# Attention and two MLPs on one Trainium2 core: weight parts of the second block pair kept in DRAM, a later touch ahead of three loads, and Silu in place of tanh for part of the first MLP

## The chip, the cores and the metric

The kernel runs on one core of a Trainium2 chip. The metric is the device time of one execution, in microseconds (us). The engines are named as the profile names them: PE is TensorE's matmul, PEld its weight load, DVE is VectorE, ACT is ScalarE, POOL is GpSimd, and SP is SyncE, which here only issues transfers (DMAs).

## What is computed

A landmark (Nystrom) attention for 4 batches, 8 heads, 576 tokens and head size 64; then a gated MLP with an RMS norm (512 to 1536 and back) and an MLP with squared ReLU (512 to 2048 and back) on all 2304 rows, in fp32.

```python
def _attn_ref(q, k, v):          # B, H, S, D = 4, 8, 576, 64; m = 32 landmarks
    q_lm = q.reshape(B, H, m, S // m, D).mean(axis=3)
    k_lm = k.reshape(B, H, m, S // m, D).mean(axis=3)
    A, Bm, C = sm(q, k_lm), sm(q_lm, k_lm), sm(q_lm, k)   # softmax of scaled products
    Z = Bm.transpose(0, 1, 3, 2) / (norm1(Bm) * norminf(Bm) + 1e-06)
    for _ in range(6):
        Z = 2 * Z - Z @ Bm @ Z
    return A @ Z @ C @ v

def _moe_ref(x, w_gate, w_val, w_out, rms_g):
    xn = x / np.sqrt(np.mean(x * x, axis=-1, keepdims=True) + 1e-06) * rms_g
    g = xn @ w_gate
    return (g * (1.0 / (1.0 + np.exp(-g)))) * (xn @ w_val) @ w_out

def _moe2_ref(x, w_in, w_out, s, b):
    r = np.maximum(x @ w_in, 0.0)
    return (s * (r * r) + b) @ w_out
```

## The kernel before, in words

**Order.** The code does not issue instructions as it is written. Each step is given to a `Scheduler` (`op`, L128) with the engines that may do it, a duration by formula, a due time (`key`) and what it reads and writes. `Scheduler.run` (L185) plays this plan once, on the host, and issues the instructions of each engine in the order that comes out; on the chip an engine then works strictly in that order and waits by semaphore. So a change of a duration, a due time or a buffer can move instructions on every engine.

**Stages.** Attention of batch 0 runs alone (to about 43 us); PE has little real work there, and plain matmuls on ones fill its gaps. From 43 to 406 us the first MLP of batch 0, 1, 2, 3 runs, and the attention of the next batch is woven into it. The first MLP's output product runs on to about 447 us. From about 416 us the second MLP begins: its 2304 rows are four blocks of 512 and one of 256, and the blocks are taken as two pairs (`pairs`, L459). From about 781 us the last block's output product ends the program.

**fp32 as two halves.** Large products are done on a rounded high part and the remainder, three matmuls for each product (`PART3`). `split` (L1228) makes both: a copy to the high part (ACT or DVE, L1230/L1231) and a subtraction (DVE or POOL, L1232).

**First MLP.** `fused` (L1419) multiplies the attention's small factor into the weights and evicts the result from two PSUM banks (L1441 to L1444). `hidden` (L1467) does, for each of 96 pieces of 128x288: the gate product into bank `pg`, ACT's `Tanh` of half of it (L1473), DVE's (tanh + 1) * gate (L1475, which reads `pg` again), the value product into `pv`, and DVE's 0.5 * that * value (L1479). Tanh and Exp share one ACT table here; the plan knows two table names, "tanh" and "sqrt", and charges `TABLE` = 1.28 us on a change. `out_mm` (L1486) is the output product, with weights loaded from DRAM (`kepto`) into a ring of two `rawo` buffers by `out_weights` (L1307).

**Second MLP, first layer.** Each pair of blocks goes through seven half-size products instead of eight (`PRODUCTS`, L1731), for 8 groups `g` of output columns (`group_of`, L1769). For this each group needs the weights' parts: three raw quarters and four sums and differences, each split in two halves. `sums` (L1382) makes them in both pairs alike: a load of 512 KB (`in_weights`, L1376), two splits into `raw` (128x1536), four differences of 128x256 (`difference`, L1327), two splits into `tot` (128x2048). `raw` and `tot` have two slots each.

**Second MLP, second layer.** `output` does the first pair and the last block; `output7` (L1875) does the second pair in seven products, with loads of stored weights: `kept5` goes straight into the weight tile `w_all`, `region` or `u_all` by a DMA on POOL's queue (L1880), `kept4` by SP.

**Start.** SP issues q, k, v of batch 0 and then the first weights. `load_gains` (L531) loads the RMS gains; on SP's queue the next loads stand behind it, a `w_val` and a `w_gate` piece first. It waits for `touch` (L535), a dummy matmul on PE that reads `gT`, and that one for the product `pY` (L766).

Of the kernel before, what the change touches and what calls it, by code (L numbers as in the profile page):

```python
# [59 lines left out]
DWELL, DWELL_FROM = 2.5, 145  # L60
ROW2, N_OUT, N_ONLY, OUT_ONLY, N_LAST = 4.0, 4.0, 4.0, 3, 1.6
# [55 lines left out]
class Scheduler:  # L117
# [67 lines left out]
    def run(self, warm):  # L185
# [10 lines left out]
        table = "tanh"  # L196
        while left:
# [61 lines left out]
            if e == "act" and o.table and o.table != table:  # L259
                table = o.table  # L260
                end += TABLE
            for b, s in self.slots_for(o).items():
                b.slot = s
                s.held = True
                if b.ring.queue:
                    b.ring.queue.remove(b)
# [36 lines left out]
def t_act(n):  # L303
    return 0.055 + 0.00085 * n
# [19 lines left out]
def tile_nystrom_attention_two_mlps(  # L324
# [131 lines left out]
    def flat(x):  # L456
        return x.rearrange("p k n -> p (k n)")
# [98 lines left out]
    def attention(b, t0, t1):  # L556
# [209 lines left out]
        if first:  # L766
            at(("pe", 0.1), pos, lambda e: touch(gT), r=[pY, "const", "top"], w=["paced"])
            load_gains(["paced"])
# [168 lines left out]
        def weighted(g, eC, rec, rc, p0):  # L937
# [14 lines left out]
            at(("pe", 0.13), p0 + 0.04, lambda e: tr(e, [4]), r=[(eC, 1), "ident", (pE[1], "taken")], w=[pE[1]])  # L952

# [428 lines left out]
    def sums(key, p, g):  # L1382
        raw, tot = Buf(raw_r), Buf(sum_r)

        def get(x, c, d, i):
# [3 lines left out]
                 "S2": get(tot, 0, 1024, 0), "S4": get(tot, 256, 1024, 0), "S1": get(tot, 512, 1024, 1), "S3": get(tot, 768, 1024, 1)}  # L1389
        r = in_weights(key, g)  # L1390
# [9 lines left out]
        for i in (1, 0):  # L1400
            c = 512 * i
            split(key + 1, lambda c=c: tot.t[:, c:c + 512], lambda c=c: tot.t[:, 1024 + c:1536 + c],
                  lambda c=c: flat(r.t)[:, c:c + 512], [(r, 2 * i), (r, 2 * i + 1)], (tot, "h", i), (tot, "l", i), 512)
        return parts
# [62 lines left out]
    def hidden(tg, tv, b, f, hf, u):  # L1467
# [5 lines left out]
        op(("act", t_act(HC)), tg, lambda e: e.activation(  # L1473
            out=th.t[:, 0:HC], in_=pg.t[:, 0:HC], func=ACTF.Tanh, scale=0.5), r=[pg], w=[th]).table = "tanh"
        op(("dve", t_dve(HC)), tg, lambda e: e.scalar_tensor_tensor(  # L1475
            out=th.t[:, 0:HC], in0=th.t[:, 0:HC], scalar=1.0, in1=pg.t[:, 0:HC], op0=ALU.add, op1=ALU.mult),
            r=[pg, th], w=[th])
        first_mm(tv, b, 1, hf, u, pv)
        op(("dve", t_dve(HC)), tv, lambda e: e.scalar_tensor_tensor(  # L1479
            out=h.t, in0=th.t[:, 0:HC], scalar=0.5, in1=pv.t[:, 0:HC], op0=ALU.mult, op1=ALU.mult),  # L1480
# [387 lines left out]
    def output7(key, m, g):  # L1868
        nm, parts, (kd, d, c), ps = OUTS7[m]
        h, j = tiles[g], pairs[1]  # L1870
        if g % 2 == 0:
# [4 lines left out]
            def load(e):  # L1876
                for i, x in enumerate(src):
                    i = slice(256 * i, 256 * i + 256)
                    if kd == 5:
                        nc.gpsimd.dma_start(out=w.t.rearrange("p (y n) -> p y n", y=2)[:, :, i], in_=x[:, :, c].bitcast(F32R))  # L1880
# [198 lines left out]
```

## Time and profile before

| | us |
|---|---|
| median of 3 runs (lowest to highest) | 807.77 (804.77 to 807.83) |
| the profiled execution, its own time | 809.28 |
| span of its instructions | 807.3 |
| PE busy | 793.0 (98%) |
| DVE busy | 673.0 (83%) |
| ACT busy | 471.7 (58%) |
| POOL busy | 159.1 (20%) |
| moved by DMA | 151 MB, mean 187 GB/s |

The clock that PE was granted is full (2.4 GHz) in all slices but the last. The span is from the first to the last instruction; what lies around it in the profiled execution's own time is 2.0 us. A sum of differences is made against this span and carried over to the median.

### The profile page before, as it was taken

Reading aid. Unit: us, or ns where it says so; the run is one execution under the profiler, and the core shown is the slowest. Engines: PE = TensorE matmul, PEld = TensorE weight load, DVE = VectorE, ACT = ScalarE, POOL = GpSimd, SP = SyncE. Lnnn points to the kernel's source line nnn. Section 1 sums busy time; section 2 is a strip of 40 time slices with the busy share of each in tenths; the row PEclk is TensorE's granted clock in tenths of the full one; section 3 lists DMA queues with packets and bytes.
Section 4 is the critical chain, followed back from the end, with each engine's and each line's share of the span. In section 5 each row is a group of like instructions: output and inputs, shape, how many; then the busy total and the mean of one; then the engine's idle time right before and its main releaser. Section 6 shows DMA issues by size and latency. Waiting matters only on the chain.

```text
span 807.3 us, 17419 instructions
## 1 busy us (share of the span) xinstructions
PE 793.0 (98%) x6475; PEld 663.6 (82%) x6475; DVE 673.0 (83%) x1489; ACT 471.7 (58%) x1000; POOL 159.1 (20%) x224
## 2 busy tenths in 40 slices
PE   8899999999999999999999999999999999999997
PEld 6587777887788878888889888877788888999996
DVE  6889997888778877898998988889798789995674
ACT  5765744453334443565557856567665577857753
POOL 1263157127311143021000000012010120022000
PEclk9999999999999999999999999999999999999999
DMA  9899998653442332499888872121866851376352
GB/s 300 291 320 357 306 290 229 220 151 99 132 132 93 108 104 92 134 288 263 279 269 270 269 233 99 40 79 39 287 221 203 286 137 66 105 175 179 92 169 80
DMA packets 101413, 151.09 MB, mean 187 GB/s; under 512 B 29264, under 2 KB 66384, under 8 KB 101328
## 3 DMA queue, kind: packets, MB, share of 16 engines
q1 hardware_dynamic: 94656, 143.55, 56.0%
q0 software_dynamic: 6528, 6.29, 3.3%
q8 instruction: 51, 0.84, 0.4%
q14 instruction: 34, 0.28, 0.1%
q10 hardware_dynamic: 144, 0.13, 0.0%
HBM read 116.91 MB, written 33.03 MB: 186 GB/s over the span
## 4 chain that ended last, share of the span: by engine, by line
PE 78%; DVE 12%; DMA 5%; ACT 2%; issue 2%; SPq 0%; POOL 0%; DVEq 0%; ACTq 0%
PE bank L1456 16%; PE bank L1412 14%; PE bank L1520 14%; PE bank L1566 11%; PE bank L1907 10%; PE bank L1816 3%; PE bank L1429 3%; DMA rawo<-kepto 2%; DMA stage<-in_moe_w_in_dram 2%; DVE w_all L1232 1%; PE bank L830 1%; PE bank L746 1%; DVE hl L1232 1%; DVE region L1232 1%; PE bank L968 1%
## 5 line engine op out<-in xcount | busy, mean ns | idle before, releaser
L1520 PE MATMUL bank<-hh,w_all 128*128 128x512 f32 (+1 forms) x472 | 155.4, 381 | 0.0
L1520 PEld LDWEIGHTS bank<-hh,w_all 128*128 128x128 f32 x472 | 86.2, 188 | 27.2 <-issue 13.1
L1520 PE MATMUL bank<-hl,w_all 128*128 128x512 f32 (+1 forms) x236 | 87.5, 371 | 1.0 <-DVE hl L1232 1.0
L1456 PE MATMUL bank<-xh,u_all 128*128 128x288 f32 x400 | 86.9, 298 | 1.1 <-DVE hbuf L1475 0.7
L1566 PE MATMUL bank<-w_all,hh 128*128 128x512 f32 x272 | 83.9, 390 | 0.0
L1473 ACT ACTIVATE hbuf<-bank 128x288 f32<-128x288 f32 x96 | 39.2, 408 | 56.9 <-PE bank L1456 56.0
L1232 DVE TENSOR_TENSOR w_all<-rawo,w_all 128x512 fp32r<-128x512 f32 x83 | 60.2, 725 | 12.5 <-ACT w_all L1230 10.0
L1456 PEld LDWEIGHTS bank<-xh,u_all 128*128 128x128 f32 x400 | 66.1, 188 | 4.7 <-DVE hbuf L1475 1.1
L1566 PEld LDWEIGHTS bank<-w_all,hh 128*128 128x128 f32 x272 | 51.0, 188 | 10.9 <-ACT hh L1230 0.4
L1456 PE MATMUL bank<-xl,u_all 128*128 128x288 f32 x200 | 58.8, 294 | 0.0
L1456 PE MATMUL bank<-xh,xl 128*128 128x288 f32 x184 | 54.2, 294 | 0.0
L1456 PE MATMUL bank<-xl,xh 128*128 128x288 f32 x184 | 54.1, 294 | 0.0
L1566 PE MATMUL bank<-w_all,hl 128*128 128x512 f32 x136 | 53.0, 390 | 0.7 <-DVE hl L1232 0.7
L1475 DVE SCALAR_TENSOR_TENSOR hbuf<-hbuf,bank 128x288 f32<-128x288 f32 x96 | 42.6, 444 | 10.8 <-ACT hbuf L1473 10.8
L1520 PEld LDWEIGHTS bank<-hl,w_all 128*128 128x128 f32 x236 | 44.5, 189 | 6.6 <-POOL region L640 1.2
L1735 ACT ACTIVATE xbuf<-xbuf,b_sb,s_sb 128x512 f32<-128x512 f32 (+1 forms) x38 | 28.8, 758 | 20.9 <-DVE xbuf L1746 20.2
L1232 POOL TENSOR_TENSOR hl<-hbuf,hh 128x288 fp32r<-128x288 f32 (+7 forms) x32 | 23.3, 732 | 87.0 <-ACT hh L1230 64.6
L1230 ACT ACTIVATE hh<-hbuf 128x288 fp32r<-128x288 f32 (+8 forms) x74 | 27.4, 395 | 21.0 <-PE bank L1520 13.8
L1456 PEld LDWEIGHTS bank<-xl,u_all 128*128 128x128 f32 x200 | 37.6, 188 | 0.8
L1230 ACT ACTIVATE w_all<-rawo 128x512 fp32r<-128x512 f32 x45 | 28.2, 626 | 17.0 <-PE bank L1520 11.2
L1412 PE MATMUL bank<-region,xh 128*128 128x512 f32 x144 | 35.9, 394 | 0.6 <-ACT hbuf L1753 0.3
L1232 DVE TENSOR_TENSOR hl<-xbuf,hh 128x512 fp32r<-128x512 f32 (+5 forms) x45 | 27.9, 624 | 10.3 <-ACT hh L1230 9.5
(395 smaller groups left out, 2110.0 us busy)
## 6 DMA issues: line engine op xcount, KB each, us to landing
rawg<-keptg SPq DMA_DIRECT2D x36, 512.0 KB, 5.1
stage<-in_moe_w_out_dram SPq DMA_DIRECT2D x28, 511.8 KB, 5.5
rawo<-kepto SPq DMA_DIRECT2D x48, 256.0 KB, 3.4
rawg<-kept SPq DMA_DIRECT2D x24, 512.0 KB, 4.3
stage<-in_moe_w_in_dram SPq DMA_DIRECT2D x15, 512.0 KB, 5.0
rawo<-kept SPq DMA_DIRECT2D x27, 256.0 KB, 3.3
keptg<-rawg SPq DMA_DIRECT2D x12, 512.0 KB, 5.6
kept<-tail SPq DMA_DIRECT2D x24, 256.0 KB, 5.3
```

Of the source, the lines that this page charges most:

```text
L1230: e.activation(out=hi(), in_=src(), func=ACTF.Copy) if e is nc.scalar
L1232: b = op({"dve": t_dve(n), "pool": t_pool(n)}, key, lambda e: e.tensor_tensor(out=lo(), in0=src(), in1=hi().bitcast(F32), op=ALU.subtract) ...
L1412: nc.tensor.matmul(out=ps.t, lhsT=a[h][:, 128 * kd:128 * kd + 128], rhs=x[kd][y].t, start=(first and kd == 0 and i == 0), stop=(last and k ...
L1429: nc.tensor.matmul(out=pU[g].t[m, 256 * j:256 * j + 256], lhsT=gw[b].t[p, m], rhs=r.t[p, :, 128 * k:128 * k + 128], start=True, stop=True)
L1456: nc.tensor.matmul(out=ps.t[:, 0:HC], lhsT=u[a].t[:, 256 * g + 128 * part:256 * g + 128 * part + 128], rhs=x[y].t.rearrange("p k n -> p (k ...
L1473: op(("act", t_act(HC)), tg, lambda e: e.activation(out=th.t[:, 0:HC], in_=pg.t[:, 0:HC], func=ACTF.Tanh, scale=0.5), r=[pg], w=[th]).tabl ...
L1475: op(("dve", t_dve(HC)), tg, lambda e: e.scalar_tensor_tensor(out=th.t[:, 0:HC], in0=th.t[:, 0:HC], scalar=1.0, in1=pg.t[:, 0:HC], op0=ALU ...
L1520: nc.tensor.matmul(out=A[c].t[:, 0:n], lhsT=w[a].t[:, 128 * c:128 * c + 128], rhs=hs[y].t[:, 0:n], start=(f == 0 and i == 0), stop=(f == F ...
L1566: nc.tensor.matmul(out=A[c].t, lhsT=hs[a].t[:, s], rhs=w.t[:, 512 * y:512 * y + 512], start=(f == 0 and i == 0), stop=(f == F2 - 1 and i = ...
L1735: e.activation(out=h.t[:, c:c + n], in_=h.t[:, c:c + n], func=ACTF.Identity, scale=s_sb, bias=b_sb) if e is nc.scalar
L1816: nc.tensor.matmul(out=ps.t[:, 0:n], lhsT=tot.t[:, 1024 * a + c:1024 * a + c + 128], rhs=xs[3, kd // 2][y].t[:, n * (kd % 2):n * (kd % 2) ...
L1907: nc.tensor.matmul(out=A.t[:, 256 * k:256 * k + 256], lhsT=hs[x].t[:, t], rhs=w.t[:, 512 * y + w0:512 * y + w0 + 256], start=(fresh and k ...
```

## The change

Five edits:

1. `sums`: in the first pair every group's finished `raw` (768 KB) and `tot` (1 MB) are also stored to DRAM (`kept6`, `kept7`); in the second pair a group loads these two instead of the 512 KB of weights, and its splits and differences fall away.
2. `output7`: the `kept5` loads are issued by SP instead of POOL.
3. The touch ahead of the gains' load, and so the gains, a `w_val` and a `w_gate` piece behind it on SP's queue, waits for the transposes of the first attention half (`pE[1]`) instead of `pY`.
4. `hidden`: where the plan finds no exp near, ACT does `Silu` of the whole gate and DVE's (tanh + 1) * gate is not issued.
5. `Scheduler.run`: a third table name, "silu"; it changes to it when the sqrt table is in, when no exp is left, or when the next exps are not ready and not due soon. Each change is charged 1.28 us.

```diff
@@
+KEPT_LEAD = 4.0
+KEY0, EXP_AFTER = 39.0, 10.0
...
@@ Scheduler.run
+        self.exps = [o for o in self.ops if o.table == "tanh"]
...
-            if e == "act" and o.table and o.table != table:
+            if e == "act" and o.table == "silu":
+                if table != "silu" and (table == "sqrt" or not self.exps or (
+                        all(x.n_deps for x in self.exps) and min(x.key for x in self.exps) + KEY0 > at + EXP_AFTER)):
+                    table = "silu"
+                    end += TABLE
+                o.form(table == "silu")
+            elif e == "act" and o.table and o.table != table:
                 table = o.table
                 end += TABLE
+            if o in self.exps:
+                self.exps.remove(o)
...
@@ attention
         at(("pe", 0.26), pos, lambda e: diag(pY, 32, 32, block(BT), block(BT)), r=[BT], w=[pY])
-        if first:
-            at(("pe", 0.1), pos, lambda e: touch(gT), r=[pY, "const", "top"], w=["paced"])
-            load_gains(["paced"])
...
             at(("pe", 0.13), p0 + 0.04, lambda e: tr(e, [4]), r=[(eC, 1), "ident", (pE[1], "taken")], w=[pE[1]])
+            if first and g == 0:
+                at(("pe", 0.1), p0 + 0.04, lambda e: touch(gT), r=[pE[1], "const", "top"], w=["paced"])
+                load_gains(["paced"])
...
@@ sums
+        if p:
+            for i, x, n in ((6, raw, 1536), (7, tot, 2048)):
+                op(("sp", t_dma(n // 2)), key - KEPT_LEAD, lambda e, i=i, x=x: e.dma_start(out=x.t.bitcast(F32), in_=kept[i, g]),
+                   r=[("k%d" % i, g)], w=[(x, y, j) for y in "hl" for j in range(2)])
+            return parts
         r = in_weights(key, g)
...
+        for i, x, n in ((6, raw, 1536), (7, tot, 2048)):
+            kept[i, g] = dr.tile([128, n], F32, name=f"kept{i}_{g}")
+            op(("sp", t_dma(n // 2)), key + 8, lambda e, i=i, x=x: e.dma_start(out=kept[i, g], in_=x.t.bitcast(F32)),
+               r=[(x, y, j) for y in "hl" for j in range(2)], w=[("k%d" % i, g)])
         return parts
...
@@ hidden
-        op(("act", t_act(HC)), tg, lambda e: e.activation(
-            out=th.t[:, 0:HC], in_=pg.t[:, 0:HC], func=ACTF.Tanh, scale=0.5), r=[pg], w=[th]).table = "tanh"
-        op(("dve", t_dve(HC)), tg, lambda e: e.scalar_tensor_tensor(
+        o = op(("act", t_act(HC)), tg, lambda e: e.activation(
+            out=th.t[:, 0:HC], in_=pg.t[:, 0:HC], func=ACTF.Silu if silu else ACTF.Tanh, scale=1.0 if silu else 0.5),
+            r=[pg], w=[th])
+        o.table, silu = "silu", False
+        d = op(("dve", t_dve(HC)), tg, lambda e: None if silu else e.scalar_tensor_tensor(
             out=th.t[:, 0:HC], in0=th.t[:, 0:HC], scalar=1.0, in1=pg.t[:, 0:HC], op0=ALU.add, op1=ALU.mult),
             r=[pg, th], w=[th])
+
+        def form(x):
+            nonlocal silu
+            silu = x
+            if x:
+                d.alts = {"dve": 0.0}
+
+        o.form = form
...
-            out=h.t, in0=th.t[:, 0:HC], scalar=0.5, in1=pv.t[:, 0:HC], op0=ALU.mult, op1=ALU.mult),
+            out=h.t, in0=th.t[:, 0:HC], scalar=1.0 if silu else 0.5, in1=pv.t[:, 0:HC], op0=ALU.mult, op1=ALU.mult),
...
@@ output7
-                        nc.gpsimd.dma_start(out=w.t.rearrange("p (y n) -> p y n", y=2)[:, :, i], in_=x[:, :, c].bitcast(F32R))
+                        e.dma_start(out=w.t.bitcast(F32).rearrange("p (y n) -> p y n", y=2)[:, :, i], in_=x[:, :, c])
```

The built programs show what the plan makes of it. DVE: of 96 instructions of the kind (tanh + 1) * gate 34 stay; differences (L1328) fall from 131 to 104 on DVE and from 13 to 8 on POOL, subtractions of a split from 410 to 388 and from 63 to 53; DVE has 1376 instructions for 1491. ACT: seven `ACT_TABLE_LOAD` more (three for exp, four for Silu), 19 copies of a split fewer. SP: 16 stores and 24 + 16 loads more, 8 loads of 512 KB fewer. PE has the same products; one filling matmul falls away.

PE at the start, before: `tail` matmuls (L746) are `pY`, `ones` with `gT` is the touch, `ident` with `region` are the transposes.

```order
L746 MATMUL bank5_68<-tail_113 32x32 x8
L536 LDWEIGHTS ones_72
L536 MATMUL bank7_70<-gT_77,ones_72 128x128
L945 MATMUL bank4_67<-ident_71,region_109 128x128 x4
L945 MATMUL bank6_69<-ident_71,region_109 64x128
```

The same place now:

```order
L757 MATMUL bank5_68<-tail_113 32x32 x8
L953 MATMUL bank4_67<-ident_71,region_109 128x128 x4
L953 MATMUL bank6_69<-ident_71,region_109 64x128
L547 LDWEIGHTS ones_72
L547 MATMUL bank7_70<-gT_77,ones_72 128x128
```

The touch moved behind the five transposes.

DVE at the first pieces of the first MLP, before: L1207 ends the attention's output, L1475 and L1479 are the piece in banks 5 and 6, L1444 evicts the next fused weights from banks 7 and 4.

```order
L1207 TENSOR_TENSOR xl0_84<-tail_113,xh0_82 128x288 x2
L1475 SCALAR_TENSOR_TENSOR hbuf_104<-hbuf_104,bank5_68 128x288
L1479 SCALAR_TENSOR_TENSOR hbuf_104<-hbuf_104,bank6_69 128x288
L1444 TENSOR_TENSOR xl0_84<-bank7_70,xh0_82 128x256
L1444 TENSOR_TENSOR xl0_84<-bank4_67,xh0_82 128x256
```

The same place now (L1509 is what L1479 was, L1462 and L1464 evict the fused weights):

```order
L1218 TENSOR_TENSOR xl0_84<-tail_113,xh0_82 128x288 x2
L1462 CAST xh0_82<-bank4_67 128x256
L1464 TENSOR_TENSOR xl0_84<-bank7_70,xh0_82 128x256
L1464 TENSOR_TENSOR xl0_84<-bank4_67,xh0_82 128x256
L1509 SCALAR_TENSOR_TENSOR hbuf_104<-hbuf_104,bank6_69 128x288
```

The eviction of bank 7 and a copy that ACT did stand ahead of the piece; on PE the third gate product moved from bank 5 to bank 7, and on ACT a table load now stands ahead of the first piece's activation.

SP while the first MLP's output product runs on its last block, before: `rawo` from `kepto` are that product's weights, `stage` are second-MLP weights to be prepared.

```order
L1314 DMA rawo0_89<-kepto0_118 128x512
L1669 DMA kept2_5_145<-tail_113 128x256
L1670 DMA kept2_5_145<-tail_113 128x256
L1378 DMA rawg1_87<-kept2_3_141 128x1024
L1314 DMA rawo1_90<-kepto1_120 128x512
L1314 DMA rawo0_89<-kepto2_122 128x512
L1266 DMA stage2_93<-in_moe2_w_in_dram 128x4x512
L1314 DMA rawo1_90<-kepto3_124 128x512
L1659 DMA kept3_3_147<-tail_113 128x512
L1261 DMA stage0_91<-in_moe2_w_out_dram 128x2047
L1314 DMA rawo0_89<-kepto4_126 128x512
```

The same place now:

```order
L1422 DMA kept7_0_163<-xh1_83 128x2048
L1325 DMA rawo1_90<-kepto1_120 128x512
L1422 DMA kept6_1_164<-u_all_96 128x1536
L1325 DMA rawo0_89<-kepto2_122 128x512
L1389 DMA rawg1_87<-kept2_3_141 128x1024
L1277 DMA stage1_92<-in_moe2_w_in_dram 128x4x512
L1325 DMA rawo1_90<-kepto3_124 128x512
L1422 DMA kept7_1_165<-xl1_85 128x2048
L1325 DMA rawo0_89<-kepto4_126 128x512
```

Stores of 1 MB, 768 KB and 1 MB stand directly ahead of the second, third and fifth of the twelve weight loads; one more of 768 KB stands ahead of the eleventh. On PE there, 78 matmuls of the second MLP's first layer now stand among the twelve output products, where 66 stood.

## Rows read from the trace of the kernel before

**Rows 1.** Stretches: length, busy us (instructions) by engine, clock, DMA share, GB/s.

```profile
43.00:460.00 417.00, 414.17 (x3994) 341.34 (x3994) 355.51 (x887) 218.76 (x540) 118.83 (x169) 1.00 0.67 208
460.00:690.00 230.00, 227.64 (x1042) 187.39 (x1041) 200.68 (x352) 152.02 (x255) 20.11 (x21) 1.00 0.47 154
```

**Rows 2.** PE's waits in the span: who ended them, total us, times, longest.

```profile
PE bank L968 <- issue: 1.5, 1, 1.5
...
PE bank L1412 <- DVE tail L1757: 1.1, 2, 0.6
PE bank L1520 <- DVE hl L1232: 1.0, 2, 0.8
...
PE bank L1566 <- DVE hl L1232: 0.7, 1, 0.7
...
PE bank L1087 <- DVE xbuf L1479: 0.4, 1, 0.4
PE bank L1456 <- DVE tail L793: 0.4, 1, 0.4
...
PE bank L1412 <- ACT hbuf L1753: 0.3, 1, 0.3
```

**Rows 3.** Timeline of the start: start us, us, engine, line, what [idle before].

```profile
18.12 0.23 PE L536 MATMUL bank<-gT,ones 128*128 128x128 bf16 x1
...
18.49 0.77 PE L945 MATMUL bank<-ident,region 128*128 128x128 f32 x5
...
18.85 0.51 SPq L1266 DMA_DIRECT2D xbuf<-in_moe_w_val_dram  x1
...
25.98 0.69 PE L968 MATMUL bank<-region 128*32 128x64 f32 x25 [1.53 <-issue]
```

**Rows 4.** DMA: the 18.85 load (us to landing); instruction packets, MB, share in 23.6:24.7.

```profile
xbuf<-in_moe_w_val_dram SPq DMA_DIRECT2D x1, 512.0 KB, 5.0
...
q8 instruction: 1, 0.02, 5.4%
```

**Rows 5.** Groups by line over the span, and a timeline row of a table load.

```profile
L1475 DVE SCALAR_TENSOR_TENSOR hbuf<-hbuf,bank 128x288 f32<-128x288 f32 x96 | 42.6, 444 | 10.8 <-ACT hbuf L1473 10.8
L1473 ACT ACTIVATE hbuf<-bank 128x288 f32<-128x288 f32 x96 | 39.2, 408 | 56.9 <-PE bank L1456 56.0
...
28.10 1.28 ACT L1046 ACT_TABLE_LOAD   x1
29.39 0.20 ACT L1046 ACTIVATE spare<-spare 128x1 f32<-128x1 f32 x1
```

**Rows 6.** Timeline at the first MLP's first pieces, DVE and PE.

```profile
42.61 0.46 DVE L1475 SCALAR_TENSOR_TENSOR hbuf<-hbuf,bank 128x288 f32<-128x288 f32 x1
...
43.12 0.40 PE L1456 MATMUL bank<-xh,u_all 128*128 128x288 f32 x1 [0.72 <-DVE hbuf L1475]
...
43.54 0.42 DVE L1444 TENSOR_TENSOR xl<-bank,xh 128x256 fp32r<-128x256 f32 x1
```

**Rows 7.** DMA of 411:447, and the chain of waits there by line.

```profile
q1 hardware_dynamic: 5591, 8.97, 79.6%
...
rawo<-kepto SPq DMA_DIRECT2D x11, 256.0 KB, 4.1
...
by line: DMA rawo<-kepto 47.6%; DVE w_all L1232 15.1%; DMA rawo<-kept 12.9%; DVE w_all L1231 6.5%; issue 6.1%; DVE tail L1285 5.5%; DVE hl L1232 3.9%; DVE xh L1232 3.6%; DVE hh L1231 2.4%; ACT w_all L1230 1.8%; DVE xl L1232 1.7%; DVE xbuf L
```

**Rows 8.** The chain of waits: twelve matmuls of L1412 on PE, and its last piece on PE.

```profile
473.10 2.72 PE bank L1412 x12
...
781.36 21.80 PE bank L1566 x96
```

**Rows 9.** Stretches of 20 us, columns as in the first group.

```profile
60.00:80.00 20.00, 19.48 (x208) 14.78 (x207) 18.15 (x49) 11.63 (x29) 7.12 (x12) 1.00 1.05 353
...
540.00:560.00 20.00, 19.20 (x83) 14.92 (x82) 19.76 (x32) 13.94 (x25) 4.90 (x4) 1.00 0.08 23
580.00:600.00 20.00, 20.00 (x90) 16.57 (x89) 18.66 (x35) 12.41 (x21) 1.62 (x2) 1.00 0.75 266
```

## The prediction

> **What bounds the kernel now.** I read the stretches by stage first. From 43 to 460 us PE is busy 414.17 of 417.00 us, from 460 to 690 us 227.64 of 230.00 us, and its clock is full [rows 1]. What can be won there is the difference: 2.8 us and 2.4 us. PE's last product ends at 781.36 + 21.80 = 803.16 us [rows 8]; the 4.1 us behind it are the last store, which the change does not touch. Before 43 us busy shares say nothing, since PE fills its gaps with matmuls on ones; there the chain of waits decides, and it goes through PE's small products. So the kernel is bound by PE's work, which the change leaves as it is, and the question is only which of PE's waits go and which come. The second view is PE's own waits [rows 2]. The largest is 1.5 us at the product L968 in the start. In the first MLP DVE ends 1.0 + 0.4 + 0.4 us [rows 2] and, at the very first pieces, 0.7 us [rows 6]. In the second MLP 1.1 + 0.7 us are ended by DVE and 0.3 us by ACT [rows 2]. That is the whole purse: 1.5 + 1.8 + 0.7 + 2.1 = 6.1 us.
>
> **Part by part.**
>
> *Loads held at the start.* The L968 wait of 1.53 us ends at 25.98 us with "issue": no engine ended it [rows 3]. Between 23.6 and 24.7 us one packet of the instruction queue moved [rows 4], the only one between 20.9 us and there; I read the wait as PE's code coming late. The `w_val` load issued at 18.85 us landed 5.0 us later, at 23.85 [rows 3, 4]. So the code packet moved just when that load was done, as if it stood behind it. The touch ran at 18.12 us; now it follows the transposes, which end at 18.49 + 0.77 = 19.26 [rows 3], 1.1 us later, and the gains, the `w_val` and the `w_gate` piece with it. If the code packet then goes in ahead of the `w_val` load, that load's own time in the queue is saved: 524 KB at 353 GB/s [rows 9], 1.5 us, about the whole wait, and the chain of the start runs through that product. Bounds: 0 (the packet does not stand behind this load) and -1.5 us. I take **-1.2 us**, since the packet still has to move and the load is only 1.1 us late. That the loads come 1.1 us later costs nothing that I see: the start takes these pieces up last. *A page speaks against this term:* the Trainium skill, "DMA: Bandwidth & Descriptors", section on queues, rings and completion order, says that a DMA engine goes round-robin between the queues that have work, packet by packet. By it the code packet would wait for a few packets and not for a load; the trace's packet, which moved as the load ended, does not bear this out, but one packet is thin. By that rule this term is 0.
>
> *The first Silu.* The sqrt table is in, so the plan changes to "tanh" and then to "silu". A load takes 1.28 us [rows 5]. At the first pieces, the next gate product on PE waited for L1475 to free bank 5, until 43.12 us [rows 6]. Now it goes to bank 7, and in L1475's place on DVE, 0.46 us, stand a copy and the eviction L1464 that frees this bank, 0.42 us each [rows 6]: 0.84 - 0.46 = 0.38 us later. The table load stands on ACT meanwhile, and banks 5 and 6 are not asked for until two products later. So PE waits **+0.4 us** more. Bounds: 0, and +1.3 if the whole load falls on the chain.
>
> *Silu in the first MLP.* 62 of 96 instructions of 444 ns leave DVE, 27.5 us [rows 5], where DVE is busy 355.51 of 417 us [rows 1]. ACT's own instruction stays one of 128x288 at 408 ns [rows 5]; Silu itself is not in the trace, and I take the same. ACT gains six more loads, 6 x 1.28 = 7.7 us, with 198 us idle [rows 1]. Most of the 27.5 us was hidden behind PE. What it can free is the 1.8 us that DVE ended; against it stand the six loads, each of which delays a piece or an exp by 1.28 us. Bounds: -1.8 and, if three of six show on PE in full, +3.8. I take **-0.8 us**, nearer the row of waits, since ACT idles half the time. *A page's price:* the Trainium skill, "ScalarE: Activation LUTs", section on what ACT_TABLE_LOAD costs, gives 2.66 us for a switch, a drain of about 1.38 us included, and tells to batch by table. By it ACT would pay 16 us for the six, and the +3.8 would be +8.0. The trace shows no drain: the load begins at 28.10 and the next activation at 29.39 [rows 5], so the trace decides.
>
> *Stores in the first pair.* Of 14 MB of stores, `kept7_0`, `kept6_1`, `kept7_1` and `kept6_2` (3.67 MB) stand among the twelve weight loads of the last output product (411 to 447 us). This is the price I fear. DMA is busy 79.6% of these 36 us, and 47.6% of the chain of waits there is the landing of `kepto` loads [rows 7]: PE had no wait, but the loads came just in time. At 353 GB/s [rows 9] the stores take 10.4 us; 7.3 us of DMA time are idle (20.4% of 36), and PE has 12 matmuls more to do meanwhile, 2.7 us [rows 8]. Lower bound: 10.4 - 7.3 - 2.7, about 0.4 us. Upper bound: no idle time is used, 10.4 - 2.7 = 7.7 us. I take **+1.5 us**, near the lower end, because the plan interleaves products where it saw a load come late. The other 10 MB lie in 460 to 560 us, where DMA is mostly idle (23 GB/s in 540 to 560 [rows 9]): nothing.
>
> *The second pair without sums.* Eight groups lose four splits of two instructions and four differences each. DVE was the engine that PE waited for at the change of pairs: it is busy 19.76 of 20 us in 540 to 560 us [rows 9], and 2.1 us of PE's waits lie in this MLP [rows 2]. The first groups of the second pair were prepared just there. I take **-1.3 us**; bounds -2.1 and 0 (the pair's own splits and differences of x stay, and they alone may fill DVE). Each group loads 1.75 MB for 0.5: in the busiest stretch 266 GB/s [rows 9] becomes 266 + 1.31 MB / 20 us = 330 GB/s, under the 353 that 60 to 80 us shows. So no wait; if there is one, up to 2 us.
>
> *`kept5` on SP.* POOL waited with these loads for PE to free a weight tile, with nothing urgent behind it. The same wait is now on SP, where the loads for later products queue behind it, but the plan puts them in order of readiness. 0; up to +1 us.
>
> Sum: -1.2 + 0.4 - 0.8 + 1.5 - 1.3 = -1.4 us. The span becomes 805.9, the profiled execution 807.9, and the median 807.77 - 1.4 = **806.4 us**.
>
> **The rivals.**
>
> *All relief, no price.* Every wait in question goes and the stores fit: -1.5 - 1.8 - 2.1 + 0.4 = -5.0: 802.8 us. For it: ACT and DMA have idle time. Against it: a new order brings new small waits.
>
> *The loads are late (slower).* One mechanism: SP's queue lands in order, and each store of 1 MB or 768 KB pushes the `kepto` load behind it by 2.8 or 2.1 us; the two `rawo` buffers make every second load wait for the one before last, so the delays add up to the upper bound, 7.7 us. With the other terms at -2.9 the time is 807.77 + 4.8 = 812.6 us. It decides against the kernel from 2.9 us on, and against the forecast's sign by over 0.5% from 6.9 us on. For it: the chain there is loads. Against it: 78 instead of 66 matmuls stand there to fill.
>
> *The hold does nothing.* The code packet moves when it moves, whatever load is in the queue; that is how it would be if the queues take turns (the Trainium skill, section named above). The first term is 0 and the rest holds: 807.6 us. For it: one packet is all the evidence for the other reading. Against it: that packet's time.
>
> *The change doesn't do what it says.* The built program shows stores, loads and Silu where the text says; left is that the tables thrash. It would be within 0.5%.
>
> **How the numbers follow.** 0.5% of 807.77 is 4.0 us, about what a measurement of this kernel can tell from no change. Forecast 0.47, all relief 0.23, late loads 0.15, hold does nothing 0.12, not as it says 0.03. Faster by over 0.5%: all relief and a sliver of the forecast's spread, 0.27. Slower: the late loads, 0.15. Same: 0.58. The range reaches from a little below "all relief" (802.0) to short of the late loads (811.0); about 1 in 10 is left out on either side.
>
> **What would show it.** Right: the wait at L968 shrinks to about 0.3 us; the third gate product starts later against the first; DVE has 62 instructions of L1475's kind fewer and ACT ten table loads in all of 1.28 us, none ended by a drain; PE's waits at 540 to 570 us fall under 1 us; `kepto` loads land 1 to 2 us later than the median 4.1. Wrong: PE waits of several us on `w_all` between 411 and 460 us, or waits on `raw` or `tot` in the second pair, would make it slower; a start that is more than 2 us shorter would make it faster than I say.

## The result and the profile after

The changed kernel takes 813.89 us (median of 8 runs, 810.93 to 817.95) for 807.8 us before, a ratio of 1.007 with a 95% interval of 1.0043 to 1.0096: 0.7% slower, where 806.4 us was forecast and the range ended at 811.0. The profiled execution took 817.71 us, 3.8 us over that median; before, it took 809.28 us. So of the 8.7 us between the two spans 2.3 us (3.8 - 1.5) belong to the two executions and not to the kernels.

The head of the page after: busy us and share of the span.

```profile
span 816.0 us, 17259 instructions
PE 796.7 (98%) x6474; PEld 666.0 (82%) x6474; DVE 628.3 (77%) x1374; ACT 465.3 (57%) x977; POOL 128.7 (16%) x184
```

DVE lost 44.7 us of work, POOL 30.4 us, ACT 6.4 us, and the kernel is slower. The stages of [rows 1], after:

```profile
43.00:460.00 417.00, 408.35 (x3939) 333.92 (x3938) 331.53 (x814) 215.30 (x527) 110.22 (x158) 0.99 0.67 211
460.00:690.00 230.00, 229.23 (x1047) 190.04 (x1045) 170.93 (x295) 140.38 (x232) 8.82 (x8) 1.00 0.72 254
```

From 43 to 460 us PE is idle for 8.7 us instead of 2.8, and its mean clock is 0.99; from 460 to 690 us it is idle for 0.8 us instead of 2.4. One stage lost and the other won. PE's waits after (who ended them, total us, times, longest), to be held against [rows 2]:

```profile
PE bank L1449 <- DVE hbuf L1509: 2.7, 2, 2.1
PE bank L1476 <- DVE xl L1464: 1.8, 1, 1.8
PE bank L1550 <- DVE hl L1243: 1.7, 2, 1.0
...
PE bank L1550 <- DVE w_all L1242: 1.1, 2, 0.9
PE bank L1449 <- DVE rawg L1296: 0.7, 1, 0.7
...
PE bank L1432 <- ACT hbuf L1783: 0.6, 1, 0.6
```

The 1.5 us at L968 (now L979) are gone, and so are the 1.1 and 0.7 us of the second MLP. New are 2.7 us at L1449, the products that multiply the attention's factor into the weights. Longer are the waits at L1476, the gate product (1.8 us, where L1456 had 0.7 us before), and at L1550, the output product (2.8 us, where L1520 had 1.0 us).

Where the time went is read by adding up PE's products (without the filling ones), each at the usual distance to the next of its kind (512 columns 224 ns, 288 columns 126 ns, 256 columns 113 ns, narrow ones 7 ns), and asking at what time each kernel has done as much as the kernel before had at a given time. How much later that is, its lag, stands in the first row, in us, and below it the same for the eleven experiments (their edits stand in the next section); each row is from one profiled execution, and the differences below are taken before rounding:

| kernel | at 48 | 120 | 150 | 400 | 467 | 540 | 592 | 800 us |
|---|---|---|---|---|---|---|---|---|
| changed kernel | 0.8 | 2.8 | 7.7 | 7.3 | 11.8 | 11.5 | 8.3 | 8.4 |
| hold_only | 1.0 | 1.0 | -0.5 | -0.7 | -0.2 | -0.2 | 0.5 | 0.4 |
| silu_only | -1.6 | 0.4 | 5.4 | 4.6 | 6.2 | 6.0 | 6.0 | 6.1 |
| kept_only | 0.3 | -0.9 | -2.4 | -2.3 | 0.0 | -0.2 | -3.4 | -3.4 |
| no_silu | 1.5 | 1.0 | -0.5 | -0.7 | 0.7 | 0.5 | -2.7 | -2.7 |
| plan_tanh | -1.7 | 0.2 | 5.2 | 4.5 | 6.3 | 6.0 | 3.0 | 2.9 |
| silu_late | -1.9 | -3.1 | -4.6 | -4.6 | -2.1 | -2.4 | -5.4 | -5.5 |
| kept_first4 | 2.8 | 2.9 | 1.5 | 1.3 | 1.3 | 1.0 | -2.3 | -2.3 |
| kept_last4 | -1.9 | -2.8 | -4.2 | -4.4 | -4.2 | -4.3 | -3.2 | -3.2 |
| pool_short | -1.8 | -0.7 | -0.8 | -1.4 | 2.6 | 2.3 | -0.8 | -0.8 |
| best | 2.5 | 2.0 | 0.5 | 0.3 | 4.6 | 4.3 | 1.2 | 1.2 |
| kept_pool5 | -1.8 | -2.9 | -4.4 | -4.4 | -2.8 | -2.7 | -5.8 | -5.9 |

Behind 48 us four stretches move: 48 to 120 us (+2.0 in the changed kernel), 120 to 150 us (+5.0), 400 to 467 us (+4.5) and 540 to 592 us (-3.1). Elsewhere behind 48 us the lag of no kernel moves by more than 0.8 us: what is lost or won on PE in one stretch is kept to the end. The eight kernels without Silu there all gain the same 1.5 us between 120 and 150 us, whatever their edit, and four of them have the order of the kernel before there: its profiled execution lost the 1.5 us by itself (its 0.8 us at L1520 of [rows 2] among them). Against these eight the changed kernel loses 6.5 us there.

The largest is seen in the trace of the changed kernel. DVE, POOL and PE from 138 to 145 us (start us, us, engine, line, what, idle before):

```profile
138.96 1.33 DVE L1243 TENSOR_TENSOR w_all<-rawo,w_all 128x512 fp32r<-128x512 f32 x1 [0.21 <-ACT w_all L1241]
140.21 0.88 DVE L1242 CAST hh<-hbuf 128x224 fp32r<-128x224 f32 x1
141.12 2.39 DVE L1243 TENSOR_TENSOR hl<-hbuf,hh 128x224 fp32r<-128x224 f32 x2
143.44 0.94 DVE L1296 SCALAR_TENSOR_TENSOR rawo<-stage,cmag_all 128x512 int32<-128x512 int32 x1
144.30 0.81 DVE L1509 SCALAR_TENSOR_TENSOR hbuf<-hbuf,bank 128x288 f32<-128x288 f32 x2
```

```profile
137.39 3.56 POOL L1218 TENSOR_TENSOR xl<-tail,xh 128x288 fp32r<-128x288 f32 x4 [2.52 <-ACT xh L1216]
140.92 1.45 POOL L651 TENSOR_TENSOR region<-region 128x576 f32<-128x576 f32 x1
142.45 2.11 POOL L655 TENSOR_TENSOR region<-region 128x256 f32<-128x256 f32 x3
```

```profile
142.04 0.62 PE L1449 MATMUL bank<-rawg,gw 64*32 64x256 f32 x2
144.80 1.72 PE L1449 MATMUL bank<-rawg,gw 64*32 64x256 f32 x30 [2.14 <-DVE hbuf L1509]
```

The two subtractions L1243 of 128x224 take 2.39 us; one that stands at 129.27 us, with POOL idle, takes 0.38 us. DVE's instructions here run in the gaps that POOL's leave, and the piece L1509, whose bank PE needs, is last in the row. PE stands for 2.14 us. If each of DVE's instructions between 120 and 150 us is held against the median of its kind and shape in all thirteen profiles, they last 6.1 us too long in sum; in the kernel before it is 1.1 us. What follows the wait costs nearly as much again: the granted clock in stretches of 2 us (length, busy us by engine, clock, DMA share, GB/s).

```profile
140.00:142.00 2.00, 2.00 (x17) 1.88 (x15) 1.97 (x3) 0.66 (x2) 2.00 (x2) 1.00 0.92 293
142.00:144.00 2.00, 0.66 (x3) 0.14 (x2) 2.00 (x3) 0.00 (x0) 1.76 (x4) 1.00 0.84 274
144.00:146.00 2.00, 1.20 (x30) 0.61 (x30) 1.11 (x3) 0.00 (x0) 0.88 (x2) 0.78 0.50 179
146.00:148.00 2.00, 2.00 (x18) 1.26 (x5) 1.40 (x5) 0.66 (x2) 0.00 (x0) 0.50 0.98 189
148.00:150.00 2.00, 2.00 (x11) 1.69 (x10) 1.72 (x6) 0.92 (x3) 0.11 (x1) 0.87 1.04 362
```

Behind the wait the clock falls to 0.50, that is 1.2 GHz, and is full again from about 148.5 us; the missing shares, 2 us x (0.22 + 0.50 + 0.13), are 1.7 us.

### The profile page after: what moved, and what is told of

Same layout as the page of the kernel before. It is cut to its first block, busy times and chain, and to the rows that moved or that the text cites. A ratio compares the mean times of both kernels' runs of the same rounds, so it can differ in the third digit from the quotient of the medians.

```text
span 816.0 us, 17259 instructions
## 1 busy us (share of the span) xinstructions
PE 796.7 (98%) x6474; PEld 666.0 (82%) x6474; DVE 628.3 (77%) x1374; ACT 465.3 (57%) x977; POOL 128.7 (16%) x184
## 4 chain that ended last, share of the span: by engine, by line
PE 84%; DVE 10%; DMA 4%; issue 1%; ACT 1%; DVEq 0%; SPq 0%; ACTq 0%
PE bank L1476 18%; PE bank L1432 16%; PE bank L1550 16%; PE bank L1596 12%; PE bank L1937 10%; PE bank L1846 3%; PE bank L1449 3%; DMA rawo<-kepto 2%; PE bank L838 1%; DMA keptg<-rawg 1%; PE bank L757 1%; DVE w_all L1243 1%; PE bank L979 1%; DVE hl L1243 1%; PE bank L820 1%
## 5 line engine op out<-in xcount | busy, mean ns | idle before, releaser
L1550 PE MATMUL bank<-hh,w_all 128*128 128x512 f32 (+1 forms) x472 | 156.1, 383 | 1.3 <-DVE w_all L1242 1.1
L1550 PEld LDWEIGHTS bank<-hh,w_all 128*128 128x128 f32 x472 | 86.8, 189 | 29.5 <-issue 13.7
L1476 PE MATMUL bank<-xh,u_all 128*128 128x288 f32 x400 | 89.1, 302 | 1.9 <-DVE xl L1464 1.8
L1550 PE MATMUL bank<-hl,w_all 128*128 128x512 f32 (+1 forms) x236 | 87.8, 372 | 1.7 <-DVE hl L1243 1.7
L1243 DVE TENSOR_TENSOR w_all<-rawo,w_all 128x512 fp32r<-128x512 f32 x86 | 61.9, 720 | 14.7 <-ACT w_all L1241 12.0
L1476 PEld LDWEIGHTS bank<-xh,u_all 128*128 128x128 f32 x400 | 67.5, 191 | 5.7 <-DVE xl L1464 2.0
L1476 PE MATMUL bank<-xl,u_all 128*128 128x288 f32 x200 | 59.6, 298 | 0.0
L1476 PE MATMUL bank<-xh,xl 128*128 128x288 f32 x184 | 54.2, 294 | 0.0
L1476 PE MATMUL bank<-xl,xh 128*128 128x288 f32 x184 | 54.1, 294 | 0.0
L1550 PEld LDWEIGHTS bank<-hl,w_all 128*128 128x128 f32 x236 | 44.8, 190 | 7.1 <-DVE hl L1243 2.2
L1241 ACT ACTIVATE hh<-hbuf 128x288 fp32r<-128x288 f32 (+9 forms) x85 | 31.9, 402 | 21.7 <-PE bank L1550 18.1
L1243 DVE TENSOR_TENSOR hl<-hbuf,hh 128x288 fp32r<-128x288 f32 (+9 forms) x75 | 37.8, 520 | 7.4 <-ACT hh L1241 7.0
L1243 DVE TENSOR_TENSOR hl<-xbuf,hh 128x512 fp32r<-128x512 f32 (+5 forms) x45 | 30.4, 677 | 12.6 <-ACT hh L1241 12.1
L1476 PEld LDWEIGHTS bank<-xl,u_all 128*128 128x128 f32 x200 | 38.2, 191 | 0.9
L1476 PEld LDWEIGHTS bank<-xl,xh 128*128 128x128 f32 x184 | 34.6, 188 | 0.8
```

The lines of the kernel that those rows point to most:

```text
L1241: e.activation(out=hi(), in_=src(), func=ACTF.Copy) if e is nc.scalar
L1243: b = op({"dve": t_dve(n), "pool": t_pool(n)}, key, lambda e: e.tensor_tensor(out=lo(), in0=src(), in1=hi().bitcast(F32), op=ALU.subtract) ...
L1476: nc.tensor.matmul(out=ps.t[:, 0:HC], lhsT=u[a].t[:, 256 * g + 128 * part:256 * g + 128 * part + 128], rhs=x[y].t.rearrange("p k n -> p (k ...
L1550: nc.tensor.matmul(out=A[c].t[:, 0:n], lhsT=w[a].t[:, 128 * c:128 * c + 128], rhs=hs[y].t[:, 0:n], start=(f == 0 and i == 0), stop=(f == F ...
```

## The experiments

Each kernel ran beside the kernel before on the same chip; ratios are to that, with their 95% interval. The line numbers of an experiment can differ by a few from those of the changed kernel.

**One edit alone, and all without Silu.** hold_only keeps of the change this:

```diff
-        if first:
-            at(("pe", 0.1), pos, lambda e: touch(gT), r=[pY, "const", "top"], w=["paced"])
-            load_gains(["paced"])
...
+            if first and g == 0:
+                at(("pe", 0.1), p0 + 0.04, lambda e: touch(gT), r=[pE[1], "const", "top"], w=["paced"])
+                load_gains(["paced"])
```

> The kernel before with one edit alone: the touch waits for the transposes (edit 3). Theory S (the Silu plan costs the time between 40 and 146 us, the hold is worth what it shows at the first gate product): that product starts at 38.9 us for 40.5, the 1.6 us stay, and the time is 806.2 us for 807.8. Theory H (the shorter start is taken back where DMA is at its limit, 43 to 130 us): the gain is gone by 170 us and the time is 807.8 us or more, up to 812.

Measured: 808.56 us, ratio 1.0011 (0.9994 to 1.0029). The hold brings nothing that can be measured: the 806.2 us of theory S lie outside the interval. But the gain was not taken back later, as theory H has it: in this profile the wait was never gone.

```profile
23.95 0.43 PE L978 MATMUL bank<-region 128*32 128x64 f32 x16
25.60 0.68 PE L978 MATMUL bank<-region 128*32 128x64 f32 x24 [1.21 <-issue]
```

silu_only is the kernel before with the edits to `hidden` and `Scheduler.run`.

> The kernel before with Silu in the first MLP alone (edits 4 and 5). Theory S: PE waits over 1.5 us at the third gate product, its clock falls behind it, and the time is 807.8 + 5 to 9 = 813 to 817 us. Theory H: the Silu plan is close to free, PE's products at 170 us are within 1.5 us of before, and the time is 807 to 809 us.

Measured: 815.08 us, ratio 1.01 (1.0082 to 1.0118). This edit is the loss. Theory S is right on the time and wrong on the place: the wait at the third gate product is 1.0 us and no clock falls there. The largest loss is at 120 to 150 us (5.0 us), with the same 2.7 us at the product of L1449 (L1440 here) as in the changed kernel. In this kernel, without the hold, the wait at L968 is gone:

```profile
24.09 0.90 PE L979 MATMUL bank<-region 128*32 128x64 f32 x40
```

kept_only is the kernel before with the stored parts and the `kept5` loads on SP.

> The kernel before with the stored parts of the second layer's weights alone (edits 1 and 2). Both theories: nothing changes before 400 us; the stores among the output product's loads cost 4.5 us between 407 and 466 us, the second pair without sums gives 3.4 us back between 540 and 575 us, the time is 807.8 + 1.1 = 808.9 us. If the gain were missing without the other edits: 812.3 us.

Measured: 805.09 us, ratio 0.9961 (0.9937 to 0.9984). A gain of 0.4%, 2.7 us, where a loss of 1.1 us was expected: in the profile 2.3 us are lost from 400 to 467 us and 3.1 us won from 540 to 592 us.

no_silu is the changed kernel with its decision for Silu taken out:

```diff
-                if table != "silu" and (table == "sqrt" or not self.exps or (
-                        all(x.n_deps for x in self.exps) and min(x.key for x in self.exps) + KEY0 > at + EXP_AFTER)):
-                    table = "silu"
+                if table != "tanh":
+                    table = "tanh"
                     end += TABLE
-                o.form(table == "silu")
+                o.form(False)
```

> The changed kernel without Silu: Tanh and (tanh + 1) * gate in all 96 pieces, the hold and the stored parts stay. Theory S: 807.8 - 1.6 + 1.1 = 807.3 us. Theory H: as slow as the changed kernel, 812 to 814 us.

Measured: 805.29 us, ratio 0.9973 (0.9955 to 0.9991). Theory S stands in its main point, Silu costs 813.9 - 805.3 = 8.6 us. It falls in its part on the hold, and the stored parts give more than it expected.

**What in the Silu edit costs the time.** plan_tanh changes one word, so that the plan is the same and only the table loads go:

```diff
-            out=th.t[:, 0:HC], in_=pg.t[:, 0:HC], func=ACTF.Silu if silu else ACTF.Tanh, scale=1.0 if silu else 0.5),
+            out=th.t[:, 0:HC], in_=pg.t[:, 0:HC], func=ACTF.Tanh, scale=1.0 if silu else 0.5),
```

> The changed kernel with its order of work kept to the last instruction, but ACT issues Tanh where it issued Silu, so that its seven added table loads fall away (62 of 96 pieces are then not computed as in the reference). Theory L (the loads of 1.28 us are what costs): the 7 us lost before 150 us go, 805 to 808 us. Theory O (the order that the plan found is what costs: DVE's turn comes too late for PE's banks): PE's waits of 2 us at 142 to 145 us stay and the time is 811 to 814 us.

Measured: 813.39 us, ratio 1.0068 (1.0041 to 1.0095). The loads cost 0.5 us, less than the interval can tell from nothing; the rest of the loss comes with the order. The wait between 125 and 148 us is unchanged without them:

```profile
PE bank L1449 <- DVE hbuf L1509: 2.7, 2, 2.2
```

silu_late lets the plan choose Silu only from 160 us on:

```diff
-                if table != "silu" and (table == "sqrt" or not self.exps or (
+                if table != "silu" and at > 160 and (table == "sqrt" or not self.exps or (
```

> The changed kernel with Silu only from 160 us on. If the whole loss is made at the two places before 150 us and Silu is free where PE does not wait: as without Silu, 805.3 us, with PE's lag constant between 160 and 400 us. If each table load costs part of its 1.28 us wherever it stands: 808 to 811 us. If DVE's saved 27 us are worth something: under 804 us.

Measured: 803.74 us, ratio 0.9947 (0.9921 to 0.9974). The whole loss lies ahead of 160 us. On the chip the first load for Silu now stands at 196.7 us; the changed kernel had Silu from 40.6 to 69.5, from 117.8 to 153.3 and from 208.7 us on. Between 160 and 400 us PE is idle for 0.24 of 240 us with Silu and 0.12 of 240 us in no_silu, though DVE has 182.24 instead of 199.57 us to do: DVE's saved work was hidden behind PE in full. That the time is just under the 804 us named for a gain does not show one: the interval takes in the time of no_silu.

```profile
160.00:400.00 240.00, 239.76 (x2438) 198.16 (x2439) 182.24 (x478) 119.04 (x311) 54.55 (x82) 1.00 0.52 165
```

pool_short keeps the order of the changed kernel and makes POOL's instructions beside the slow place shorter:

```diff
+            N = 4 if b == 2 else D
...
-                out=y(), in0=x()[:, 0:9], in1=x()[:, 9:18], op=ALU.add),
+                out=y()[:, :, 0:N], in0=x()[:, 0:9, 0:N], in1=x()[:, 9:18, 0:N], op=ALU.add),
...
-                    out=y()[:, 0:n], in0=y()[:, 0:n], in1=y()[:, n:2 * n], op=ALU.add), r=[tmp], w=[tmp], pair=True)
+                    out=y()[:, 0:n, 0:N], in0=y()[:, 0:n, 0:N], in1=y()[:, n:2 * n, 0:N], op=ALU.add), r=[tmp], w=[tmp], pair=True)
```

> The changed kernel with the same order of work, but POOL's sums of the third batch's landmarks (lines 651 and 655) take 4 of 64 columns (60 are left out, so that this batch's attention is wrong). Theory P (DVE's instructions between 138 and 145 us last up to three times as long because POOL's run beside them, and PE's wait behind them is theirs): the waits at the product of line 1449 fall from 2.7 us to under 1 us, the clock stays full at 144 to 150 us, and the time is 813.9 - 3.5 to 6 = 808 to 810.5 us. Theory Q (the order alone makes DVE late, POOL is beside it by chance): the waits stay over 2 us and the time is 812.5 to 814.5 us.

Measured: 807.82 us, ratio 0.9994 (0.9975 to 1.0013): 6.1 of Silu's 8.6 us are back. The row of DVE there, and what is left of PE's waits between 125 and 150 us:

```profile
133.90 1.34 DVE L1245 TENSOR_TENSOR w_all<-rawo,w_all 128x512 fp32r<-128x512 f32 x1 [0.22 <-ACT w_all L1243]
135.16 0.88 DVE L1244 CAST hh<-hbuf 128x224 fp32r<-128x224 f32 x1
136.08 0.78 DVE L1245 TENSOR_TENSOR hl<-hbuf,hh 128x224 fp32r<-128x224 f32 x2
136.79 0.68 DVE L1298 SCALAR_TENSOR_TENSOR rawo<-stage,cmag_all 128x512 int32<-128x512 int32 x1
137.40 0.81 DVE L1511 SCALAR_TENSOR_TENSOR hbuf<-hbuf,bank 128x288 f32<-128x288 f32 x2
```

```profile
PE bank L1451 <- DVE hbuf L1511: 0.3, 1, 0.3
```

Ahead of POOL's shortened sums the first two rows are as slow as in the changed kernel (1.34 and 0.88 us, beside POOL's long subtractions); beside the shortened sums the pair of subtractions takes 0.78 instead of 2.39 us. PE's wait of 2.1 us is gone, the clock stays at 1.00, and the lag grows by 0.0 us between 120 and 150 us instead of 5.0. DVE's instructions there last 3.3 us too long in sum instead of 6.1. Nor is it that POOL's results come earlier: between 100 and 150 us DVE waits for no instruction of POOL in either kernel. Theory P stands, with a time 0.2 us under its range. It takes both, the order and POOL beside it: in the kernels without Silu there, with POOL's sums in full, DVE's instructions last 1.1 to 2.0 us too long. The other 2.5 us of the 8.6 are open. In the profiles the four kernels with Silu there lose 1.0 to 2.0 us between 48 and 120 us, with PE waits of 0.7, 0.6 and 0.5 us that DVE ends, where no kernel without it loses more than 0.2; no run takes these waits apart.

**Where the stored parts pay.** kept_first4 and kept_last4 are kept_only with half of the groups:

```diff
-        if p:
+        if p and g < 4:
...
-        for i, x, n in ((6, raw, 1536), (7, tot, 2048)):
+        for i, x, n in () if p or g >= 4 else ((6, raw, 1536), (7, tot, 2048)):
             kept[i, g] = dr.tile([128, n], F32, name=f"kept{i}_{g}")
```

> Edits 1 and 2 alone, with stored parts for groups 0 to 3 only; groups 4 to 7 make their sums in both pairs. If the relief lies at the change of pairs (PE's waits at 540 to 570 us): the stores' 2.4 us and the gain of 3.4 us both stay, 805 to 806 us. If it is spread over the eight groups: 807.8 + 2.4 - 1.7 = 808.5 us.

Measured: 805.12 us, ratio 0.9943 (0.9917 to 0.9969).

> Edits 1 and 2 alone, with stored parts for groups 4 to 7 only, so that no store stands among the twelve loads of the output product. If the relief lies at the change of pairs: neither cost nor gain, 807 to 808 us, and PE's waits of about 2 us at 540 to 570 us stay. If it is spread over the groups: 807.8 - 1.7 = 806.1 us.

Measured: 807.87 us, ratio 0.9996 (0.9973 to 1.0019). This time alone would also fit the 806.1 us; the 808.5 us for kept_first4 are excluded by its interval. The relief lies at the change of pairs: with the first four groups stored, the profile shows no wait of PE between 535 and 590 us; with the last four, the waits there are

```profile
PE bank L1431 <- DVE tail L1786: 1.1, 2, 0.5
PE bank L1431 <- DVE xbuf L1786: 0.8, 1, 0.8
PE bank L1595 <- DVE hl L1242: 0.7, 1, 0.7
PE bank L1431 <- DVE region L1242: 0.2, 1, 0.2
```

The four stores among the output product's loads stand in the same places in kept_only and kept_first4, and PE's order is the same up to 490 us. Yet 2.3 us are lost from 400 to 467 us in the one profiled execution and nothing in the other, so the order does not set this cost. With one profile for each kernel it stays open whether it differs between executions of one kernel.

kept_pool5 is kept_only with the `kept5` loads back on POOL:

```diff
-                        e.dma_start(out=w.t.bitcast(F32).rearrange("p (y n) -> p y n", y=2)[:, :, i], in_=x[:, :, c])
+                        nc.gpsimd.dma_start(out=w.t.rearrange("p (y n) -> p y n", y=2)[:, :, i], in_=x[:, :, c].bitcast(F32R))
```

> Edit 1 alone: as edits 1 and 2, but the kept5 loads are issued by POOL as before. If it does not matter which queue issues them: 805.1 us, the same as with SP. If SP's order costs something behind 690 us: 804 us; if POOL's costs: over 806 us.

Measured: 804.47 us, ratio 0.9955 (0.993 to 0.998), beside 0.9961 with SP: no difference. PE, DVE and ACT have the order of kept_only to the last instruction, and yet the wait at L968, 1.98 us there, is absent here. The two kernels at that product, kept_only first:

```profile
23.93 0.42 PE L978 MATMUL bank<-region 128*32 128x64 f32 x15
26.33 0.69 PE L978 MATMUL bank<-region 128*32 128x64 f32 x25 [1.98 <-issue]
```

```profile
23.99 0.90 PE L978 MATMUL bank<-region 128*32 128x64 f32 x40
```

**Both gains together.** best is kept_first4 with Silu from 160 us on.

> Stored parts for groups 0 to 3 only, Silu only from 160 us on, the touch where it was. The two gains lie at different places (540 to 575 us, and whatever Silu gave after 160 us), so they add up: 802.5 to 804.5 us. If Silu after 160 us is worth nothing: 805 us.

Measured: 806.48 us, ratio 0.9981 (0.9957 to 1.0005). They do not add up. The profiled execution took 810.24 us, 3.8 us over the median, so not all that it shows belongs to the kernel. Its lag grows by 4.3 us from 400 to 467 us, where kept_first4's stands still; waits at the output product (`hl`, 1.3 us) and at the first product of the second MLP (ACT, 1.3 us) make up most of it. Silu in the last pieces of the first MLP changes the order there again. But one and the same order, in the changed kernel, plan_tanh and pool_short, lost 4.5, 1.8 and 4.0 us there, so what the order costs in this stretch is not shown. The fastest kernels are silu_late, kept_pool5, kept_only and kept_first4, 0.4 to 0.6% ahead of the kernel before, and their intervals overlap.

## Why the prediction was wrong, by its own steps

*Loads held at the start (-1.2).* The failed step is "as if it stood behind it". The second code packet moved at 20.1 to 21.4 us in seven of the thirteen profiled executions and at 23.3 to 24.8 us in six, and only in these six does PE wait at that product (1.2 to 2.6 us, and the first gate product starts at 40.5 to 43.3 instead of 38.6 to 38.9 us). Early it was with the hold (four of six) and without it (three of seven), so the hold alone does not set it, and hold_only's time shows no gain. The order of work does not set it either: kept_only and kept_pool5 have the same and differ. One profile was read as if its wait came with every execution; that it differs between executions of one kernel is likely (29 of the kernel before on one chip took 805.1 to 812.4 us) but not shown, as each kernel has only one profile. The rival that the hold does nothing was right on this term. What decides when the packet moves is open; that it waits only for the queues' turns, packet by packet, as the Trainium skill has it ("DMA: Bandwidth & Descriptors", section on queues, rings and completion order), no run here shows or excludes.

*The first Silu (+0.4).* PE waited there for 0.72 us before. In silu_only, plan_tanh and pool_short it was 1.0 us with a full clock, 0.3 us more, as forecast; in the changed kernel's profile it was 1.79 us, and the clock fell to 0.50 behind it. The step (a copy moves from ACT to DVE because the table load stands on ACT) is what the trace shows. The larger size in the one execution has a second part: DVE stood for 0.68 us at L1296 for a store to land. So 0.4 us was right in three profiles of four, and this is not where the time went.

*Silu in the first MLP (-0.8, bounds -1.8 and +3.8).* This is the step that failed the sum: without and with this edit are 805.3 and 813.9 us, +8.6, over twice the upper bound. The price was sought in the table loads, and they cost nothing that can be measured: plan_tanh has none of the seven and takes 0.5 us less, within its interval. They took 1.28 us each, ten in all. ACT's next instruction began 0.01 us behind a load in seven of the ten, with no drain, as forecast; so the 2.66 us of the Trainium skill ("ScalarE: Activation LUTs", section on what ACT_TABLE_LOAD costs) do not hold here. What was put at nothing is that a plan with other durations is another order on every engine; the prediction names new small waits only as an argument against a rival. In that order DVE's subtractions and copies in SBUF stand beside POOL's sums, PE waits behind them, and 6.1 of the 8.6 us go when these sums are short. The trace of before could have been asked: L1285, 0.69 us elsewhere, lasts 1.87 us there beside POOL's 2.82 us from 42.70 us on.

```profile
44.21 1.87 DVE L1285 SCALAR_TENSOR_TENSOR rawg<-stage,cmag_all 128x512 int32<-128x512 int32 x1
```

*Stores in the first pair (+1.5, bounds 0.4 and 7.7).* In kept_first4, kept_pool5 and kept_only, which have these stores without the hold or Silu, 0.0, 1.5 and 2.3 us are lost from 400 to 467 us: near the 1.5 us on the mean, but the 0.0 lies under the lower bound, and hold_only loses 0.6 us there without any store. The changed kernel lost 4.5 us there, and silu_only 1.6 us without any store. (The sixteen stores are 14.7 MB and not 14; the sum uses only the four.) The late `kepto` load that was feared is there once or twice, as in the changed kernel:

```profile
446.34 0.43 DVE L1242 CAST w_all<-rawo 128x512 fp32r<-128x512 f32 x1 [1.95 <-DMA rawo<-kepto]
```

but the delays did not add up to the 7.7 us: PE's waits on `w_all` there are 1.3 us in all. The rival of late loads gave 812.6 us, near the measured 813.9, by the wrong mechanism; that is luck.

*The second pair without sums (-1.3, bounds -2.1 and 0).* The mechanism and its place were right and the size was off: 3.0 to 3.3 us won in all nine kernels that load the parts of the first groups, beyond the bound of 2.1 us. The purse was taken from the listed waits (2.0 us). But a listed wait begins where the matmul before has ended, while the next one could have started before that: at 564.9 us PE's next product starts about 860 ns later than at the usual distance, and the list has 680 of them. Waits under 0.15 us are not listed. The stretch of 35 us behind 540 us shows it, before and in kept_only: PE's busy time grows by 1.9 us, but it does 13 products more, which at 224 ns are 2.9 us.

```profile
540.00:575.00 35.00, 32.94 (x140) 25.37 (x139) 32.25 (x54) 25.65 (x45) 5.85 (x5) 1.00 0.26 81
540.00:575.00 35.00, 34.87 (x153) 28.26 (x152) 29.40 (x48) 25.48 (x43) 3.92 (x3) 1.00 0.51 158
```

The loads of 1.75 MB for a group are hidden, as forecast. *`kept5` on SP (0)*: right.

Of the signs to look for, most of those of the parts came true (62 fewer of L1475's kind, ten loads of 1.28 us, no wait at 540 to 570 us, a later third gate product). The L968 wait was gone too, but not by the hold: that was luck. The `kepto` loads landed 0.7 us later (4.8 us), not 1 to 2. The sum did not come true: the list had no sign for the places that it took for safe, between 100 and 150 us.

## What to carry to other kernels

Work taken from an engine that PE does not wait for can be worth nothing: between 160 and 400 us DVE had 17 us less to do, and PE's idle time did not fall (0.24 for 0.12 us). Where a scheduler makes the order, the new order can cost more than all the parts of the edit together: look for the places where the engine that PE waits for has SBUF work beside POOL's, and keep the edit away from there, as silu_late did. To tell the cost of an operation from the cost of the order that it brings, keep the order and swap the operation. And before a wait of one profile goes into a sum, look whether a second profile has it, of the same program or of one with the same order there.

## What the runs showed of the hardware

Some of DVE's instructions with all operands in SBUF do not run beside POOL's, those with two inputs there and copies (CAST) among them. When POOL's began first, DVE's ends only behind it. In the changed kernel a subtraction of 0.38 us takes 1.2 us, a copy of 128x224 takes 0.88 us (0.27 us in the kernel before), and an instruction on 96x6 numbers, usually 0.16 us, takes over 1 us:

```profile
130.16 1.19 DVE L1252 SCALAR_TENSOR_TENSOR tail<-tail 96x6 f32<-96x6 f32 x1
131.38 1.37 DVE L1253 SCALAR_TENSOR_TENSOR tail<-tail 96x6 f32<-96x6 f32 x1
```

These two end within 0.03 us of POOL's instructions, 1.30 us from 130.03 and 1.44 us from 131.28 us. When DVE's began first, POOL's takes longer: DVE's subtraction of 128x512 at 77.37 us keeps its 0.68 us, and POOL's of 128x224 from 77.41 us takes 1.16 us (0.67 us at 53.33 us).

Two kinds of DVE's instructions keep their time beside POOL. One is those that read a bank of PSUM: two of L1464 take 0.75 us at 137.85 us, with POOL busy from 137.39 to 140.95 us, as they do alone at 127.57 us (0.76 us). The other is sums along a row and transpositions: two sums lie here within POOL's L651 (1.42 us from 104.05 us) and take 0.46 and 0.44 us, and one at 290.73 us with POOL idle takes 0.46 us; a transposition of 128x1152 takes 1.34 us at 134.19 us, partly beside POOL, and 1.37 us alone at 172.32 us.

```profile
137.85 0.75 DVE L1464 TENSOR_TENSOR xl<-bank,xh 128x256 fp32r<-128x256 f32 x2
104.29 0.46 DVE L1025 TENSOR_REDUCE tail<-tail 128x9 f32<-128x288 f32 x1
104.99 0.44 DVE L1025 TENSOR_REDUCE tail<-tail 128x9 f32<-128x288 f32 x1
```

The Trainium skill, "SBUF — State Buffer", section "SBUF: two separate sides", says that DVE and GpSimd share a pair of ports, and that of GpSimd's instruction and one of DVE with two SBUF inputs or in a two-port mode the one that starts first holds it for its whole time; the trace agrees. So Silu, which removes a DVE instruction that reads a bank, leaves DVE with a larger share of those that POOL can block; whether that share by itself costs time was not tried.

A wait on PE can cost nearly twice its length, by the clock. Behind 1.79 us at 42.55 us and behind 2.14 us at 144.80 us in the changed kernel the granted clock fell to 0.50 (1.2 GHz), for 1.7 us of lost work in the second case; behind waits of 1.0 us in silu_only and plan_tanh it stayed full. The length of the one wait does not decide it alone: in kept_only the clock stayed full behind 1.98 us at 26.33 us, and in hold_only it fell behind 1.21 us at 25.60 us.
